# Batch 0's retention in three chains, q scaled on GpSimd and the multiply after the values taken out

## The chip, the cores and the metric

One core of a Trainium2 chip runs the whole kernel in one launch. The metric is the device time of that launch in microseconds; the kernel before takes 803.81 us (median of three runs, 803.64 to 804.98).

## The reference

The program is a retention layer (attention with a decay in place of the softmax) and two feed-forward layers behind it. Shapes: 4 batches, 8 heads, 576 positions, head size 64; then 2304 tokens of width 512.

```
scores = q @ k.T / sqrt(64)
ret    = scores * D            # D[i, j] = gamma_h ** (i - j) for i >= j, else 0
attn   = ret @ v               # heads side by side: x, 2304 x 512
h      = (x @ w1) * (x @ w2) @ w3        # 512 -> 1024 -> 1024
x      = h @ w_out                       # 1024 -> 512
g      = max(x @ w_in, 0) + alpha * min(x @ w_in, 0)   # 512 -> 2048
out    = g @ w_out2                      # 2048 -> 512
```

The feed-forward weights come in float64 and are split on the core into a high and a low float32 part; x is split the same way, and each product is made of three matmuls (high x high, high x low, low x high).

## The kernel before

**Retention.** Heads are treated in pairs, one head on partitions 0 to 63, the other on 64 to 127; a batch has four pairs. Positions go in four chunks of 128 and a tail of 64 (`NCH = 5`). With the decay written as `gamma**i * gamma**-j`, a chunk needs: `scores` (TensorE, L287, L276), a multiply by a mask that holds `gamma**-j` and the causal zeros (VectorE, L291, L279, tiles `rt`, `rte`), `moments` (k times v of the chunk, L302, after the keys were scaled by ScalarE in `prep`, L265), a running state `S` that is aged by `gamma**128` and added to (VectorE, L310, L312; `gc` holds the factors), and `values` (L333: state times q; L342: masked scores times v), both into one PSUM tile `o`. Then `decayed` multiplies `o` by `qs`, which is `gamma**i / 8` for each query position (L349, into the tile `xs`), and `split` makes the high part on ScalarE (L172, `xh`) and the low part on VectorE (L173, `xl`).

The masks, the tail mask and `qs` of all pairs are one tile `per_pair`, 448 columns a pair, loaded pair by pair in `load_pair` for batch 0.

`steps()` returns six steps; step c issues scores of chunk c+1, values of chunk c and moments of chunk c+1. What follows on other engines is put in the list `later` and issued at the next `flush()`.

**Batch 0** runs before anything else, as two chains of two pairs (`r0`, `r1`), interleaved by the list `order` at L448. Sixteen matmuls on zeros come first (L440). Between steps, `ws.tick(n)` advances the weight pieces: each piece has four steps (`_first` on ScalarE L93 and L94, `_second` on VectorE L103 to L108, `_third` on ScalarE L112, `_fourth` on VectorE L116), a tick does at most one step of each kind, and the argument says up to which piece.

**Blocks.** The tokens are then cut into blocks of 512 (`BLOCKS`); `ab_unit(n, c)` multiplies a block's x by column c of w1 and of w2 (two groups of 12 matmuls, L179, tile `ps`; weight pieces 2c and 2c+1). Between the groups a `cycle` function is called: it flushes, advances the retention of the next batch, and then does a weight tick. During the first three columns of block 0 that is batch 1:

```python
r = retention(1)
between = cycle(r, 7 / 6, 1, 6)
for c in range(3):
    ws.until(2 * c + 2)
    ab_unit(0, c, between)
```

`ws.until(n)` ticks until n pieces are finished. The first step of a `retention(b)` is `prep`, so the first call of `between` issues all eight key scalings of batch 1, then a tick; the second issues its first scores and moments, then a tick. Batches 2 and 3 lie in the same way between later columns; there odd pairs are stored with the two heads swapped (`crossed`), and `cross()` rewrites the constants for that.

**Order.** TensorE, ScalarE and SyncE (which issues all DMAs) take their instructions in the order of the program text; VectorE and GpSimd are put in order by the framework's planner. After this part come two larger feed-forward stages (from L557 on), which the change does not touch.

Of the kernel before, what the change touches and what calls it, by code (L numbers as in the profile page):

```python
# [16 lines left out]
P = 128  # L17
# [120 lines left out]
def retention_moe_kernel(ctx: ExitStack, tc, qk, kv, w_out1, w3t, w12, w_in, w_out2, alpha, c_row, c_pair, out):  # L138
# [81 lines left out]
    xsp = pool(pa, "xs", bufs=2, side="left")  # L220
# [31 lines left out]
    class Retention:  # L252
# [14 lines left out]

        def scores(self, c):
# [26 lines left out]
        def moments(self, c):  # L295
# [9 lines left out]
            def state():  # L305
                new = attn.tile([P, NPAIR, D], F32, tag="S", name=f"S{b}_{c}", bufs=3)[:, 0:n]
                if c == 0:
                    nc.vector.tensor_copy(new, st)
                else:
                    nc.vector.tensor_tensor(out=new, in0=self.state[c - 1], in1=gc[:, self.ps].unsqueeze(2)  # L310
                                            .to_broadcast([P, n, D]), op=ALU.mult)
                    nc.vector.tensor_tensor(out=new, in0=new, in1=st, op=ALU.add)  # L312
                self.state = {**(self.state or {}), c: new}
# [3 lines left out]
        def values(self, c):  # L317
# [26 lines left out]
            later.append(lambda: self.decayed(c, o, w))  # L344

        def decayed(self, c, o, w):

            x = xsp.tile([P, NPAIR, CH], F32, tag="x", name=f"xs{self.b}_{c}")[:, 0:self.n, 0:w]
            nc.vector.tensor_tensor(out=x.rearrange("p (i r) w -> p i r w", r=2),  # L349
                                    in0=o[:, :, 0:self.n // 2, 0:w].rearrange("p r i w -> p i r w"),  # L350
                                    in1=qs[:, self.ps, 0:w].rearrange("p (i r) w -> p i r w", r=2), op=ALU.mult)
            t0 = self.b * S + c * CH
            cuts = [0] + [t - t0 for t, _ in BLOCKS if t0 < t < t0 + w] + [w]

            def parts():
                for lo, up in zip(cuts, cuts[1:]):
                    n = (t0 + lo) // 512
                    at = t0 + lo - BLOCKS[n][0]
                    xh, xl = (m[:, self.ps, at:at + up - lo] for m in x_block(n))
                    split(xh, xl, x[:, :, lo:up])  # L360

            later.append(parts)
# [21 lines left out]
    def cross():  # L384

        for p in range(1, NPAIR, 2):
# [3 lines left out]
            in_places(2, p, mtail[:, p], c_pair[:, p, 2 * CH:2 * CH + 64])  # L390

    def load_pair(b, p):
# [10 lines left out]
        if b == 0:  # L403
            nc.sync.dma_start(out=per_pair[:, p], in_=c_pair[:, p])
# [24 lines left out]
    nc.sync.dma_start(out=per_row, in_=c_row)  # L429
    load_pair(0, 0)  # L430
    ws.load_until(1)
    load_pair(0, 1)
    load_pair(0, 2)
# [6 lines left out]
    for _ in range(16):  # L440
        nc.tensor.matmul(warm, idle[:, 0:P], idle[:, :512], start=True, stop=True)
    r0, r1 = Retention(0, [0, 1], psum0), Retention(0, [2, 3], psum0)
    r0.prep([0])
    ws.tick(1)
    r0.prep([1])
    ws.tick(1)
    s0, s1 = r0.steps(), r1.steps()
# [682 lines left out]
```

## Time and profile before

| | |
|---|---|
| median of three runs | 803.81 us |
| profiled execution, span | 801.9 us |
| profiled execution, outside the span | not listed; the median is 1.9 us above the span |
| TensorE busy | 787.0 us, 98% |
| VectorE busy | 498.6 us, 62% |
| ScalarE busy | 348.9 us, 44% |
| GpSimd busy | 0.2 us, four instructions |
| granted clock | 0.8 of full speed in the first 40th of the span, 0.9 or more in all others |
| DMA engines | 0.9 or more busy in the first 40th, 0.8 in the second |

The span runs from the first to the last instruction of one profiled execution. Engine names in rows: PE is TensorE (PEld its weight loads), DVE VectorE, ACT ScalarE, POOL GpSimd, SPq the queue of SyncE. `L291` is line 291 of the kernel before. An arrow in brackets names what ended the idle time before an instruction.

### The profile page before, as it was taken

Reading aid. Unit: us, or ns where it says so; the run is one execution under the profiler, and the core shown is the slowest. Engines: PE = TensorE matmul, PEld = TensorE weight load, DVE = VectorE, ACT = ScalarE, POOL = GpSimd, SP = SyncE. Lnnn points to the kernel's source line nnn. Section 1 sums busy time; section 2 is a strip of 40 time slices with the busy share of each in tenths; the row PEclk is TensorE's granted clock in tenths of the full one; section 3 lists DMA queues with packets and bytes.
Section 4 is the critical chain, followed back from the end, with each engine's and each line's share of the span. In section 5 each row is a group of like instructions: output and inputs, shape, how many; then the busy total and the mean of one; then the engine's idle time right before and its main releaser. Section 6 shows DMA issues by size and latency. Waiting matters only on the chain.

```text
span 801.9 us, 12688 instructions
## 1 busy us (share of the span) xinstructions
PE 787.0 (98%) x4768; PEld 694.4 (87%) x4768; DVE 498.6 (62%) x895; ACT 348.9 (44%) x648; POOL 0.2 (0%) x4
## 2 busy tenths in 40 slices
PE   7899999999999999999999999999999999999998
PEld 4678888888888988999999999999987888888886
DVE  4895785325477799888833677587899923222232
ACT  3453562231255566656514465465666522222121
POOL 0000000000000000000000000000000000000000
PEclk8999999999999999999999999999999999999999
DMA  9843931561366669899916925225557635344341
GB/s 347 343 159 120 345 150 54 166 247 54 116 201 181 201 201 353 285 400 407 381 46 216 358 100 197 109 98 199 184 194 247 209 99 177 106 132 138 99 136 42
DMA packets 81341, 156.24 MB, mean 195 GB/s; under 512 B 9600, under 2 KB 57728, under 8 KB 81280
## 3 DMA queue, kind: packets, MB, share of 16 engines
q1 hardware_dynamic: 81280, 155.43, 55.6%
q8 instruction: 37, 0.61, 0.3%
q14 instruction: 24, 0.20, 0.1%
HBM read 104.02 MB, written 51.38 MB: 194 GB/s over the span
## 4 chain that ended last, share of the span: by engine, by line
PE 90%; DVE 4%; DMA 2%; issue 1%; ACT 1%; SPq 1%; ACTq 0%; DVEq 0%
PE ps L179 25%; PE o L1045 23%; PE h L884 18%; PE y L817 12%; PE pw L631 5%; PE sc L287 2%; PE o L342 2%; PE o L333 1%; PE st L302 1%; DMA kv<-in_kv_dram 1%; DMA xs<-x2d 1%; DMA gr<-gd 0%; DVE gl L173 0%; DVE g L902 0%; DVE g L896 0%
## 5 line engine op out<-in xcount | busy, mean ns | idle before, releaser
L179 PE MATMUL ps<-xh,w 128*128 128x512 f32 (+1 forms) x640 | 186.0, 372 | 0.6 <-DVE w L116 0.3
L1045 PE MATMUL o<-wb,gh 128*128 128x512 f32 x576 | 177.6, 389 | 1.1 <-ACT gh L172 1.1
L179 PEld LDWEIGHTS ps<-xh,w 128*128 128x128 f32 x640 | 116.0, 188 | 22.3 <-DVE w L116 0.7
L1045 PEld LDWEIGHTS o<-wb,gh 128*128 128x128 f32 x576 | 108.1, 188 | 23.8 <-ACT gh L172 1.5
L179 PE MATMUL ps<-xl,w 128*128 128x512 f32 (+1 forms) x320 | 118.0, 369 | 0.0
L1045 PE MATMUL o<-wb,gl 128*128 128x512 f32 x288 | 112.3, 390 | 0.4 <-DVE gl L173 0.4
L173 DVE TENSOR_TENSOR gl<-gr,gh 128x768 fp32r<-128x768 f32 x48 | 45.9, 957 | 100.1 <-ACT gh L172 100.1
L817 PE MATMUL y<-yab,wp 128*128 128x384 f32 x576 | 100.0, 334 | 0.0
L817 PEld LDWEIGHTS y<-yab,wp 128*128 128x128 f32 x576 | 99.9, 188 | 0.1
L172 ACT CAST gh<-gr 128x768 fp32r<-128x768 f32 x48 | 40.2, 838 | 116.5 <-PE o L1045 112.0
L179 PEld LDWEIGHTS ps<-xl,w 128*128 128x128 f32 x320 | 60.4, 189 | 9.8 <-DVE xl L173 0.3
L1045 PEld LDWEIGHTS o<-wb,gl 128*128 128x128 f32 x288 | 54.1, 188 | 12.5 <-DVE gl L173 1.3
L896 DVE SCALAR_TENSOR_TENSOR g<-m,al,g 128x384 f32<-128x384 f32 x48 | 29.7, 618 | 49.3 <-ACT g L895 47.8
L884 PE MATMUL h<-xT,wv 128*128 128x384 f32 x288 | 54.9, 334 | 1.5 <-DVE g L902 1.5
L884 PE MATMUL h<-xT,wu 128*128 128x384 f32 x288 | 55.0, 335 | 0.5 <-ACT h L909 0.3
L884 PEld LDWEIGHTS h<-xT,wv 128*128 128x128 f32 x288 | 50.3, 188 | 1.8 <-DVE g L902 1.8
L108 DVE CUSTOM_DVE_ANT_0 a<-a,b 128x1024 uint16<-128x1024 uint16 x72 | 49.5, 688 | 3.3
L884 PEld LDWEIGHTS h<-xT,wu 128*128 128x128 f32 x288 | 50.2, 188 | 1.1 <-ACT h L909 0.6
L488 ACT CAST ab<-f 128x512 fp32r<-128x512 f32 (+1 forms) x40 | 23.1, 577 | 63.8 <-DVE f L492 59.4
L492 DVE TENSOR_TENSOR f<-f,ps 128x512 f32<-128x512 f32 (+1 forms) x40 | 25.3, 632 | 30.8 <-PE ps L179 30.6
L103 DVE TENSOR_SCALAR a<-a 128x512 f32<-128x512 f32 x72 | 30.4, 422 | 22.3 <-ACT a L93 21.9
L631 PE MATMUL pw<-wo,w 128*128 128x512 f32 x192 | 43.7, 389 | 0.0
(95 smaller groups left out, 1008.8 us busy)
## 6 DMA issues: line engine op xcount, KB each, us to landing
gd<-g SPq DMA_DIRECT2D x96, 192.0 KB, 1.9
gr<-gd SPq DMA_DIRECT2D x96, 192.0 KB, 2.6
abd<-ab SPq DMA_DIRECT2D x32, 512.0 KB, 4.1
raw<-in_w_out_dram SPq DMA_DIRECT2D x24, 512.0 KB, 3.9
yab<-abd SPq DMA_DIRECT2D x24, 384.0 KB, 8.2
raw<-in_w_dram SPq DMA_DIRECT2D x16, 512.0 KB, 6.9
raw<-in_w3t_dram SPq DMA_DIRECT2D x16, 512.0 KB, 4.1
rawi<-in_w_in_dram SPq DMA_DIRECT2D x16, 512.0 KB, 6.1
```

What stands on the lines that cost most here:

```text
L103: nc.vector.tensor_scalar(out=a, in0=a, scalar1=self.LEAST, scalar2=self.MOST, op0=ALU.max, op1=ALU.min)
L108: nc.vector.tensor_tensor(out=a.bitcast(I32), in0=a.bitcast(I32), in1=b, op=ALU.add)
L172: nc.scalar.copy(hi, src)
L173: nc.vector.tensor_tensor(out=lo, in0=src, in1=_f32(hi), op=ALU.subtract)
L179: nc.tensor.matmul(ps, a, bb, start=(n == 0), stop=(n == last))
L488: nc.scalar.copy(t[:, 0], f)
L492: nc.vector.tensor_tensor(out=f, in0=f, in1=pss[1], op=ALU.mult)
L631: nc.tensor.matmul(acc[i], a[:, ic], bb, start=(k == 0 and n == 0), stop=(k == C1 - 1 and n == 2))
L817: nc.tensor.matmul(ys[o], wpc[c][a][:, oc], yab[b, c][:, bb], start=(c == 0 and i == 0), stop=(c == C1 - 1 and i == 2))
L884: nc.tensor.matmul(ps, a[:, x, ks], b[:, y, k], start=(fresh and n == 0), stop=(n == 5), skip_group_check=True)
L896: nc.vector.scalar_tensor_tensor(out=g, in0=r, scalar=neg[:, c:c + 1], in1=g, op0=ALU.mult, op1=ALU.add)
L1045: nc.tensor.matmul(accs[b][i], x[:, m, ic], y, start=(j == 0 and m == 0 and q == 0), stop=(j == C1 - 1 and m == 1 and q == 2))
```

## The change

Batch 0 is run as three chains: pair 0, pair 1, then pairs 2 and 3. The masks are loaded in two transfers of two pairs each, the first ahead of pair 0's data. q is multiplied by `qs` in place on GpSimd before the scores (two instructions a pair), so the PSUM tile `o` already holds the finished x; the multiply L349 and the pool `xs` are gone, and `parts` splits x straight from PSUM. The aging of the state is a GpSimd instruction behind the addition (`aged`), for the chunks that have a successor. For crossed batches `cross()` also rewrites `qs`. Two warm matmuls fewer are issued. In batch 0 weight piece 0 takes its four steps in the first two chains, and weight piece 1 takes all four in the third; before, piece 1 took two there and the other two in `ws.until(2)`. The loads of batch 1's pairs 0 and 1 follow the last step of the second chain.

```diff
@@ -217,7 +217,6 @@
     pa = ExitStack()
     decay = pool(pa, "decay", side="left")
     attn = pool(pa, "attn", side="left")
-    xsp = pool(pa, "xs", bufs=2, side="left")
     early = pool(pa, "early", bufs=2, side="left")
     pb = ExitStack()
     xp = pool(pb, "xp", side="right")
@@ -264,6 +263,14 @@
                 for j in range(2):
                     nc.scalar.activation(k[:, 4 * j:4 * j + 4], k[:, 4 * j:4 * j + 4], AF.Copy,
                                          scale=kd[:, 2 * p + j:2 * p + j + 1])
+
+        def scale(self, pairs=None):
+            for p in pairs or self.pairs:
+                q, by = qt[self.b][p], qs[:, p]
+                full = q[:, 0:512].rearrange("p (c i) -> p c i", i=CH)
+                nc.gpsimd.tensor_tensor(out=full, in0=full, in1=by.unsqueeze(1).to_broadcast([P, 4, CH]),
+                                        op=ALU.mult)
+                nc.gpsimd.tensor_tensor(out=q[:, 512:S], in0=q[:, 512:S], in1=by[:, 0:64], op=ALU.mult)
 
         def scores(self, c):
             b, n = self.b, self.n
@@ -307,10 +314,12 @@
                 if c == 0:
                     nc.vector.tensor_copy(new, st)
                 else:
-                    nc.vector.tensor_tensor(out=new, in0=self.state[c - 1], in1=gc[:, self.ps].unsqueeze(2)
+                    nc.vector.tensor_tensor(out=new, in0=self.aged, in1=st, op=ALU.add)
+                self.state = {**(self.state or {}), c: new}
+                if c < NCH - 2:
+                    self.aged = attn.tile([P, NPAIR, D], F32, tag="aged", name=f"aged{b}_{c}", bufs=2)[:, 0:n]
+                    nc.gpsimd.tensor_tensor(out=self.aged, in0=new, in1=gc[:, self.ps].unsqueeze(2)
                                             .to_broadcast([P, n, D]), op=ALU.mult)
-                    nc.vector.tensor_tensor(out=new, in0=new, in1=st, op=ALU.add)
-                self.state = {**(self.state or {}), c: new}
 
             later.append(state)
 
@@ -341,25 +350,23 @@
                         vj, rj = vt[b][p][rows], rt[rows, m]
                     nc.tensor.matmul(o[pp, p % 2, m // 2, 0:w], vj, rj, start=(c == 0 and m in clears), stop=True,
                                      skip_group_check=True)
-            later.append(lambda: self.decayed(c, o, w))
-
-        def decayed(self, c, o, w):
-
-            x = xsp.tile([P, NPAIR, CH], F32, tag="x", name=f"xs{self.b}_{c}")[:, 0:self.n, 0:w]
-            nc.vector.tensor_tensor(out=x.rearrange("p (i r) w -> p i r w", r=2),
-                                    in0=o[:, :, 0:self.n // 2, 0:w].rearrange("p r i w -> p i r w"),
-                                    in1=qs[:, self.ps, 0:w].rearrange("p (i r) w -> p i r w", r=2), op=ALU.mult)
+            later.append(lambda: self.parts(c, o[:, :, 0:n // 2 or 1, 0:w], w))
+
+        def parts(self, c, o, w):
+
             t0 = self.b * S + c * CH
             cuts = [0] + [t - t0 for t, _ in BLOCKS if t0 < t < t0 + w] + [w]
-
-            def parts():
-                for lo, up in zip(cuts, cuts[1:]):
-                    n = (t0 + lo) // 512
-                    at = t0 + lo - BLOCKS[n][0]
-                    xh, xl = (m[:, self.ps, at:at + up - lo] for m in x_block(n))
-                    split(xh, xl, x[:, :, lo:up])
-
-            later.append(parts)
+            for lo, up in zip(cuts, cuts[1:]):
+                m = (t0 + lo) // 512
+                at = t0 + lo - BLOCKS[m][0]
+                if self.n == 1:
+                    src = o[:, self.pairs[0] % 2, :, lo:up]
+                    xh, xl = (x[:, self.ps, at:at + up - lo] for x in x_block(m))
+                else:
+                    src = o[:, :, :, lo:up].rearrange("p r i w -> p i r w")
+                    xh, xl = (x[:, self.ps, at:at + up - lo].rearrange("p (i r) w -> p i r w", r=2)
+                              for x in x_block(m))
+                split(xh, xl, src)
 
         def steps(self):
             def step(c):
@@ -388,6 +395,7 @@
             for h in range(2):
                 nc.sync.dma_start(out=mask[:, h, p], in_=c_pair[:, p, (1 - h) * CH:(2 - h) * CH])
             in_places(2, p, mtail[:, p], c_pair[:, p, 2 * CH:2 * CH + 64])
+            in_places(2, p, qs[:, p], c_pair[:, p, 2 * CH + 64:])
 
     def load_pair(b, p):
         x = attn.tile([P, 2, S], F32, tag=f"qk{p}", name=f"qk{b}_{p}")
@@ -400,8 +408,6 @@
         else:
             nc.sync.dma_start(out=x, in_=qk[b, p])
             nc.sync.dma_start(out=y, in_=kv[b, p])
-        if b == 0:
-            nc.sync.dma_start(out=per_pair[:, p], in_=c_pair[:, p])
 
     def load_apart(b, p, n):
 
@@ -427,9 +433,11 @@
     first = ExitStack()
     psum0 = attention_psum(first, 2)
     nc.sync.dma_start(out=per_row, in_=c_row)
+    nc.sync.dma_start(out=per_pair[:, 0:2], in_=c_pair[:, 0:2])
     load_pair(0, 0)
     ws.load_until(1)
     load_pair(0, 1)
+    nc.sync.dma_start(out=per_pair[:, 2:4], in_=c_pair[:, 2:4])
     load_pair(0, 2)
     load_pair(0, 3)
     ws.load_until(2)
@@ -437,26 +445,24 @@
     load_apart(1, 2, 10)
     load_apart(1, 3, 13)
     warm = psum0["o"].tile([P, 512], F32, tag="o", name="warm", bufs=2)
-    for _ in range(16):
+    for _ in range(14):
         nc.tensor.matmul(warm, idle[:, 0:P], idle[:, :512], start=True, stop=True)
-    r0, r1 = Retention(0, [0, 1], psum0), Retention(0, [2, 3], psum0)
-    r0.prep([0])
-    ws.tick(1)
-    r0.prep([1])
-    ws.tick(1)
-    s0, s1 = r0.steps(), r1.steps()
-    order = [s0[0], s0[1], s0[2], s0[3], None, s1[0], s0[4], s1[1], s0[5], s1[2], s1[3], s1[4], s1[5]]
-    pieces = {1: 1, 6: 1, 8: 2, 10: 2}
-    for n, step in enumerate(order):
-        if step is None:
-            r1.prep()
-            continue
+    r0, r1, r2 = (Retention(0, pairs, psum0) for pairs in ([0], [1], [2, 3]))
+    s0, s1, s2 = r0.steps(), r1.steps(), r2.steps()
+
+    def ready(r, p):
+        r.scale([p])
+        r.prep([p])
+
+    def loads():
+        load_pair(1, 0)
+        load_pair(1, 1)
+
+    one, two = (lambda: ws.tick(1)), (lambda: ws.tick(2))
+    for step in (lambda: ready(r0, 0), s0[0], one, s0[1], s0[2], one, lambda: ready(r1, 1), s0[3], one, s1[0],
+                 s0[4], one, s1[1], s0[5], s1[2], s1[3], lambda: ready(r2, 2), s1[4], lambda: ready(r2, 3),
+                 s1[5], loads, s2[0], s2[1], two, s2[2], two, s2[3], two, s2[4], two, s2[5]):
         step()
-        if step is s0[-1]:
-            load_pair(1, 0)
-            load_pair(1, 1)
-        if n in pieces:
-            ws.tick(pieces[n])
         flush()
     flush()
     flush()
@@ -517,7 +523,12 @@
 
     def retention(b):
         r = Retention(b, list(range(NPAIR)), psum1)
-        return Steps([r.prep] + r.steps())
+
+        def prep():
+            r.scale()
+            r.prep()
+
+        return Steps([prep] + r.steps())
 
     first_o = ExitStack()
     psum1["o"] = pool(first_o, "ps_o1", space=PSUM, reuse_waits="tile")
```

## Rows read from the trace of the kernel before

**Rows 1.** Stages: time, busy us of engines (count), granted clock, DMA share, GB/s.
```profile
7.40:34.00 26.60, 20.92 (x290) 16.64 (x289) 19.74 (x51) 9.38 (x22) 0.00 (x0) 0.87 1.03 413
...
68.00:110.00 42.00, 41.85 (x194) 34.16 (x190) 28.39 (x53) 24.01 (x47) 0.00 (x0) 1.00 0.78 263
```

**Rows 2.** Waits of 0 to 34 us: total us, times, longest.
```profile
ACT xh L172 <- DVE xs L349: 14.7, 8, 2.7
...
PE sc L287 <- DMA qk<-in_qk_dram: 2.5, 1, 2.5
```

**Rows 3.** VectorE groups of 7.4 to 34 us, shapes apart: busy us, mean ns.
```profile
L291 DVE TENSOR_TENSOR rt<-sc,per_pair 128x512 f32<-128x512 f32 x8 | 5.5, 687 | 0.4 <-DMA per_pair<-const_pair_dram 0.3
L349 DVE TENSOR_TENSOR xs<-o,per_pair 128x256 f32<-128x256 f32 x8 | 3.3, 418 | 1.0 <-PE o L342 0.8
L173 DVE TENSOR_TENSOR xl<-xs,xh 128x256 fp32r<-128x256 f32 x7 | 3.0, 425 | 2.0 <-ACT xh L172 2.0
L310 DVE TENSOR_TENSOR S<-S,per_row 128x128 f32<-128x128 f32 x6 | 1.7, 283 | 0.0
```

**Rows 4.** Timeline of TensorE around batch 1's start, and its first wait.
```profile
10.36 0.80 PE L287 MATMUL sc<-qk 64*128 64x128 f32 x4 [2.46 <-DMA qk<-in_qk_dram]
...
33.90 0.50 PE L179 MATMUL ps<-xh,w 128*128 128x512 f32 x1
...
39.56 0.71 PE L287 MATMUL sc<-qk 64*128 64x128 f32 x8
...
42.24 0.50 PE L179 MATMUL ps<-xh,w 128*128 128x512 f32 x1 [0.18 <-ACT w L112]
...
43.27 0.50 PE L179 MATMUL ps<-xh,w 128*128 128x512 f32 x1 [0.29 <-DVE w L116]
```

**Rows 5.** Timeline of ScalarE, 37.9 to 43.3 us.
```profile
37.91 0.58 ACT L502 COPY f<-ps 128x512 f32<-128x512 f32 x1
38.38 1.71 ACT L265 ACTIVATE kv<-kv,per_row 128x256 f32<-128x256 f32 x4
39.99 1.70 ACT L265 ACTIVATE pair<-pair,per_row 128x256 f32<-128x256 f32 x4
41.59 0.61 ACT L112 CAST w<-a 128x512 fp32r<-128x512 f32 x1
```

**Rows 6.** Timeline of SyncE's DMA issues, batch 1's second pair.
```profile
26.19 0.42 SPq L401 DMA_DIRECT2D qk<-in_qk_dram  x1
26.71 0.37 SPq L402 DMA_DIRECT2D kv<-in_kv_dram  x1
```

**Rows 7.** Those two DMAs: count, KB, us from issue to landing.
```profile
qk<-in_qk_dram SPq DMA_DIRECT2D x1, 576.0 KB, 8.4
kv<-in_kv_dram SPq DMA_DIRECT2D x1, 544.0 KB, 9.2
```

**Rows 8.** Timeline of weight piece 0, first and second step.
```profile
8.98 0.66 ACT L93 ACTIVATE a<-raw 128x512 f32<-128x512 f32 x1 [0.90 <-DMA raw<-in_w_dram]
...
11.43 0.69 DVE L108 CUSTOM_DVE_ANT_0 a<-a,b 128x1024 uint16<-128x1024 uint16 x1
```

**Rows 9.** GpSimd's widest instruction, and VectorE's widest mask multiply.
```profile
0.24 0.10 POOL L1113 MEMSET const-float32-0.0<- 128x1 f32 x1 [0.24 <-issue]
...
41.40 1.22 DVE L291 TENSOR_TENSOR rt<-sc,per_pair 128x1024 f32<-128x1024 f32 x1
```

**Rows 10.** Granted clock from 9 to 17 us, columns as in Rows 1.
```profile
9.00:9.50 0.50, 0.00 (x0) 0.00 (x0) 0.00 (x0) 0.50 (x1) 0.00 (x0) 1.00 0.98 404
9.50:10.00 0.50, 0.00 (x0) 0.00 (x0) 0.33 (x1) 0.50 (x2) 0.00 (x0) 0.77 1.00 411
...
13.00:14.00 1.00, 1.00 (x9) 0.93 (x8) 1.00 (x4) 0.07 (x1) 0.00 (x0) 0.50 1.00 407
...
16.50:17.00 0.50, 0.50 (x8) 0.36 (x8) 0.50 (x3) 0.00 (x0) 0.00 (x0) 0.91 1.00 412
```

**Rows 11.** Key scaling of batches 2 and 3: ns, first and last start.
```profile
L265 ACT ACTIVATE kv<-kv,per_row x16: 497/498/512, 105.0 to 176.7; 128x256 f32<-128x256 f32 x16
```

## The prediction

> **What bounds the kernel now.** I read the table of stages first. From 68 us on TensorE is busy in practically the whole of every stretch (41.85 of 42.0 us in the first one) at the full granted clock [rows 1]; work taken from VectorE or added to GpSimd there is beside it and is worth nothing. The stretch that the change can shorten is 7.4 to 34 us, the retention of batch 0: TensorE 20.92 of 26.6 us, VectorE 19.74, granted clock 0.87 on average, and the DMA engines full (share 1.03, 413 GB/s) [rows 1].
>
> The waits say why it is long. TensorE stands 2.5 us for the second pair's q and k [rows 2, 4]; ScalarE waits 14.7 us in eight places for VectorE's `xs` [rows 2], which is one link of a chain: scores, mask multiply, values, `xs`, `xh`, `xl`, all but three on VectorE. The reader should also see what comes behind: block 0's first matmul is at 33.90, its 24 matmuls end at 39.56 where batch 1's scores begin, and the next weight column starts at 42.24 with its third matmul (the first that needs the low half of the weights) at 43.27 [rows 4]. From there TensorE runs without a wait of note to the end of batch 1. So the change is worth what it does to those two moments, 42.24 and 43.27, and not what it does to 33.90.
>
> **Batch 0 ends earlier.** Removed from VectorE: ten multiplies into `xs` (eight at 0.418, so 3.3 us, and two small ones) and six agings (6 x 0.283 = 1.7) [rows 3]. Added, because pairs 0 and 1 now run alone at half width: eight mask multiplies of 256 columns for four of 512, 8 x 0.42 - 4 x 0.687 = 0.6 (0.42 from the `xs` row, the same shape); eight low halves of 128 columns for four of 256, 8 x 0.283 - 4 x 0.425 = 0.6; up to eight state operations for four, at most 4 x 0.283 = 1.1 [rows 3]. The fourth step of weight piece 1 (0.7, a 512-wide operation as in [rows 3]) moves from behind block 0's start to before it. Net about -2 us of VectorE work, and the chain loses a link per chunk. With nothing else gained the start of block 0 goes from 33.90 to some 31.7; with most of VectorE's idle time in the stretch gone too (26.6 - 19.74 = 6.9 us, of which the first two cannot go), to 27. I take 29.5.
>
> The front of it loses a little, and is hidden. Two masks (448 KB) now stand ahead of pair 0, 224 KB more than before ahead of pair 1: at 413 GB/s [rows 1] 0.55 us for pair 1, so its q and k come at 10.9 for 10.36 [rows 4]. Then GpSimd scales q, 128x512 and 128x64. The trace has no such instruction: GpSimd's four memsets take 0.10 at 128x1, VectorE's multiply 0.69 at 128x512 and 1.22 at double width [rows 3, 9]. Bounds 0.1 and 1.22 a pair for the large part; I take 1.2, the upper one, since the lower is of one column, and 1.5 with the tail. Meanwhile pair 0's four steps fill the time in which TensorE stood 2.46 us. The two warm matmuls fewer cost nothing: TensorE waits for data there.
>
> At this place the rule of the Trainium skill against the change is weighed: GPSIMD Engine Reference, section 4.1 Engine selection, keeps elementwise work with two inputs on VectorE, GpSimd being about twice as slow. By it the estimate is 2 x 0.69 = 1.4 for the large part. No run here shows it yet; the sum would not move by it.
>
> Aging on GpSimd has a whole step of slack: the aged state is wanted when the next chunk's moment is done, one step later, and a step is at least the 0.69 of the mask multiply plus the other VectorE work. Cost nothing, up to 1.22 [rows 9], below a step of two pairs.
>
> **What batch 1 then waits for.** The queue of transfers is full throughout 7.4 to 34 us, and the change leaves its bytes and the order of the later ones as they are. So batch 1's second pair lands when it landed before: q and k at 26.19 + 8.4 = 34.6, keys and values at 26.71 + 9.2 = 35.9 [rows 6, 7]. Before, this was hidden: ScalarE scaled those keys only at 38.38 [rows 5]. Now it is late.
>
> ScalarE runs in the order written. The weight ticks are the second half of it: before, two ticks ran just ahead of block 0 (in `ws.until(2)`), and they did the first step of pieces 2 and 3 and the second step of piece 2. Now the four ticks inside the third chain have finished piece 1, `until(2)` finds nothing to do, and piece 2 begins in the first `between` call, behind the copy L502 and behind the eight key scalings of batch 1. Those are 0.43 each (1.71 for four) [rows 5]. The chain: keys land 35.9; pairs 1, 2 and 3, 6 x 0.43 = 2.58, end at 38.48; first step of piece 2 to the end of its second took 11.43 + 0.69 - 8.98 = 3.14 for piece 0 [rows 8], so 41.62; high half and the matmul 42.24 - 41.59 = 0.65 [rows 4, 5], so 42.27; low half: 0.61 for L112 [rows 5], 0.69 for a 512-wide operation of VectorE [rows 3] and 0.1 for the handovers, third matmul about 43.0. Against 42.24 and 43.27 before: +0.03 and -0.27, so **-0.25**. This holds for any start of block 0 up to 31.7, because L502 waits for half of block 0's 5.66 us (39.56 - 33.90): 31.7 + 2.83 + 0.47 (38.38 - 37.91) + 0.86 is 35.9 [rows 4, 5]. The five microseconds gained before it become a wait. Bounds on the chain: -0.5 if VectorE is free at each step, +1.2 if the planner puts batch 1's mask multiply (1.22 [rows 9]) into it.
>
> GpSimd scales four pairs here. If in order of pairs: from 34.6, three pairs at 1.5 give 39.1 and the last scores at 39.4; 42.27 is not reached before 2.3 us a pair.
>
> **The clock.** From 29.5 + 5.66 = 35.2 to 42.27 TensorE has 7.1 us, and in it only batch 1's first scores and moments, under 2.7 us before, waits included (42.24 - 39.56 [rows 4]). In the trace, TensorE stood still from 7.9 to 10.36, and the granted clock fell inside 9.5 to 10.0 (0.77 there, 0.50 after, so from 2.4 to 1.2 GHz); it was back inside 16.5 to 17.0 (0.91), TensorE having been busy without a gap from 13.0 [rows 4, 10]. By those rows the clock falls again about 40, and comes back after some 3.6 us (16.6 - 13.0) to 6.2 us (16.6 - 10.36) of work at half speed: 1.8 to 3.1 us lost. I take 2.0, near the lower end, since dense matmuls follow here.
>
> **Edits priced at nothing.** Batches 1 to 3 lose `xs` (0.69 each) and agings on VectorE, beside a full TensorE [rows 1]; before batch 2 four more small DMAs pass through SyncE's queue, at the 0.4 of an issue [rows 6] 1.6 us, and batch 2's keys are scaled at 105.0, batch 3's at 176.7 [rows 11], long after their loads; GpSimd's 6 us per batch lies in that slack. PSUM `o` is held for one cast more, with two buffers in batches 0 and 1.
>
> A second rule of the Trainium skill: SBUF — State Buffer, section Who interferes with whom, says that GpSimd and VectorE share a port pair under an exclusive lock. No row shows GpSimd reading. By it VectorE could stand 1.2 us once or twice in batch 0; block 0 would start at 31 for 29.5, still under 31.7, and the sum stays.
>
> **Sum.** Span 801.9 - 0.25 + 2.0 = 803.65; outside the span lie 1.9 us (803.81 - 801.9, the median of the three runs), so 805.6.
>
> **Rivals.**
> 1. *The wait comes, the clock holds.* For it: later in the stretch TensorE waits too and the clock stays. Against: a wait of 2.46 us did bring it down [rows 4, 10], and the one here is longer. 803.81 - 0.25 = 803.6, up to 804.8 with the mask multiply in the chain.
> 2. *Faster: block 0's early start reaches the end.* One mechanism: piece 2 is ready before TensorE wants it, because the keys land earlier or the first step of piece 2 is not behind them. Then the next column follows the last moments: 38.48 + 0.3 = 38.8 for 42.24, -3.4, so 800.4. For it: VectorE and ScalarE have the time. Against: full DMA engines and ScalarE's written order. It decides if piece 2's first step runs before 35.
> 3. *Slower: GpSimd is dear.* Above 2.3 us a pair (three times VectorE's multiply), batch 1's scores set the end: at 3 us a pair 34.6 + 9 + 0.9 = 44.5, +2.2, and the clock falls as well: 808. For it: no row prices GpSimd. Against: VectorE does the same multiply in 0.69 [rows 3], and 2.3 is over three times that.
>
> **How the numbers follow.** Forecast 0.46 (own range 804.8 to 807.2), rival 1 0.25, rival 2 0.17, rival 3 0.12. A measurement can tell about 0.2%, 1.6 us: under 802.2 is faster, over 805.4 slower. Faster: rival 2, 0.17. Slower: 0.36 of the forecast, rival 3, hardly any of rival 1: 0.48. Same: the rest, 0.35. The range 801.0 to 807.6 takes in the forecast, rival 1, the upper half of rival 2 and a third of rival 3.
>
> **What would show it.** In the profile after: block 0's first matmul at 28 to 31.7 (if later than 33, the first step is wrong); ScalarE waiting for batch 1's keys until about 35.9; L93 of piece 2 behind the eight scalings; the next weight column at 42 to 43; the granted clock at 0.5 for some microseconds after it; GpSimd's scaling near 1.2 us. A next column before 40, or a clock of 1.00 throughout 36 to 48 us, makes the prediction wrong.

## The result, and the profile after

The changed kernel takes 815.6 us (median of five runs, 814.28 to 815.71) against 803.81 for the kernel before (five runs, 803.46 to 805.7): ratio 1.0133, 95% interval 1.0115 to 1.015; it is slower by 10.7 us by the ratio, by 11.8 by the medians. The prediction was 805.6. Its sign was right; its size was not, and the time lies outside the predicted range.

Lines have moved: in the kernel after, L264 scales the keys, L271 and L273 scale q, L294 makes scores, L298 is the mask multiply, L309 makes moments, L317 adds to the state, L321 ages it, L342 and L351 make values, L508 copies a group out of PSUM.

The stages first, columns as in [rows 1]. The row 7.4 to 34 answers to the first of [rows 1], 68 to 110 to the second; the rows after them cut the first 58 us finer.

```profile
7.40:34.00 26.60, 24.88 (x239) 18.09 (x240) 17.58 (x44) 9.42 (x25) 13.99 (x22) 0.68 1.02 410
68.00:110.00 42.00, 40.63 (x290) 33.30 (x288) 23.45 (x38) 14.98 (x28) 7.46 (x8) 1.00 0.61 193
...
14.00:16.00 2.00, 2.00 (x22) 1.26 (x20) 1.75 (x3) 0.18 (x1) 1.85 (x3) 0.56 1.03 424
16.00:20.00 4.00, 4.00 (x32) 2.73 (x32) 2.37 (x9) 0.74 (x3) 1.86 (x4) 0.50 1.03 403
28.00:32.00 4.00, 4.00 (x42) 3.37 (x42) 2.93 (x6) 1.50 (x3) 1.36 (x2) 0.59 1.03 425
48.00:50.00 2.00, 0.00 (x0) 0.00 (x0) 2.00 (x4) 0.00 (x0) 0.37 (x1) 0.59 0.00 0
50.00:55.00 5.00, 3.94 (x8) 2.65 (x9) 4.86 (x11) 3.43 (x6) 0.00 (x0) 0.50 0.57 210
```

VectorE is busy 17.58 for 19.74 us in this window, but batch 0 is not over at 34. Up to block 0's first matmul (33.90 before, 37.63 after) it is busy 1.4 us more than before, 21.11 us:

```profile
7.40:37.63 30.23, 27.82 (x289) 20.17 (x289) 21.11 (x52) 10.68 (x28) 16.34 (x25) 0.72 0.99 396
```

The work itself shrank by the 2 us that the prediction took, but wide steps of the weight pieces take twice as long beside GpSimd. VectorE's groups up to block 0, first before, then after:

```profile
L106 DVE SCALAR_TENSOR_TENSOR a<-raw,a 128x512 uint32<-128x512 uint32 x2 | 1.4, 692 | 0.1
```

```profile
L106 DVE SCALAR_TENSOR_TENSOR a<-raw,a 128x512 uint32<-128x512 uint32 x2 | 2.9, 1426 | 0.0
L116 DVE TENSOR_TENSOR w<-a,w 128x512 fp32r<-128x512 f32 x2 | 2.8, 1404 | 0.0
```

L116 takes 0.68 us before. With a small one (L874, 0.85 for 0.18) these give back 3.6 us. TensorE is busier (24.88 for 20.92) and no further: its granted clock is 0.68 of full speed where it was 0.87. It runs at 0.50, that is 1.2 GHz, from about 14.3 to 31 us. Before, the low level lasted from inside 9.5 to 10 to inside 16.5 to 17 [rows 10]. It falls a second time inside 48 to 50 and stays low past 55.

TensorE's timeline, the moments of [rows 4]:

```profile
13.80 0.34 PE L309 MATMUL st<-kv 128*64 128x64 f32 x4 [1.41 <-DVE S L317]
...
37.63 0.50 PE L179 MATMUL ps<-xh,w 128*128 128x512 f32 x1
...
50.90 0.80 PE L179 MATMUL ps<-xh,w 128*128 128x512 f32 x1 [5.82 <-ACT w L112]
...
110.47 0.50 PE L179 MATMUL ps<-xh,w 128*128 128x512 f32 x1 [1.84 <-ACT f L508]
```

Against [rows 4]: block 0 starts at 37.63 for 33.90 (+3.7), the next weight column at 50.90 for 42.24 (+8.7), its second group at 58.71 for 48.34 (+10.4). A stand of 1.84 us at 108 is new. The two, 10.4 + 1.8, make the 12.0 between the spans (813.9 and 801.9) within 0.2: the loss is complete at 111 us, and a stage that starts at 422.2 before starts at 434.2.

At the first stand, at 12.4, TensorE waits for the addition L317, which needs the aged state from GpSimd. GpSimd's timeline:

```profile
10.32 1.52 POOL L271 TENSOR_TENSOR qk<-qk,per_pair 128x512 f32<-128x512 f32 x1 [0.66 <-DMA qk<-in_qk_dram]
11.81 0.76 POOL L273 TENSOR_TENSOR qk<-qk,per_pair 128x64 f32<-128x64 f32 x1
12.54 0.29 POOL L321 TENSOR_TENSOR aged<-S,per_row 128x64 f32<-128x64 f32 x1
```

Pair 0's state is aged behind pair 1's scaling, whose two instructions take 2.28 us, and is ready at 12.83. VectorE, busy without a gap from 9.63 to 13.86, adds it 0.6 us later, behind a step of a weight piece:

```profile
12.85 0.68 DVE L108 CUSTOM_DVE_ANT_0 a<-a,b 128x1024 uint16<-128x1024 uint16 x1
13.45 0.21 DVE L317 TENSOR_TENSOR S<-aged,st 128x64 f32<-128x64 f32 x1
```

So GpSimd's queue and VectorE's order both stand behind it; their shares are not shown. The second stand is read from ScalarE's timeline, whose rows answer to [rows 5]:

```profile
40.69 0.59 ACT L508 COPY f<-ps 128x512 f32<-128x512 f32 x1 [2.68 <-PE ps L179]
41.17 1.71 ACT L264 ACTIVATE kv<-kv,per_row 128x256 f32<-128x256 f32 x4
42.78 1.69 ACT L264 ACTIVATE pair<-pair,per_row 128x256 f32<-128x256 f32 x4
44.38 0.67 ACT L93 ACTIVATE a<-raw 128x512 f32<-128x512 f32 x1
...
50.23 0.62 ACT L112 CAST w<-a 128x512 fp32r<-128x512 f32 x1 [2.99 <-DVE a L108]
```

And from VectorE's, between that L93 and that L112, without a row left out:

```profile
45.08 0.43 DVE L103 TENSOR_SCALAR a<-a 128x512 f32<-128x512 f32 x1 [0.91 <-ACT a L93]
45.42 1.22 DVE L298 TENSOR_TENSOR rt<-sc,per_pair 128x1024 f32<-128x1024 f32 x1
46.55 0.42 DVE L104 TENSOR_SCALAR a<-a 128x512 uint32<-128x512 uint32 x1
46.89 0.42 DVE L315 COPY S<-st 128x256 f32<-128x256 f32 x1
47.22 0.68 DVE L490 TENSOR_TENSOR ab<-f,ab 128x512 fp32r<-128x512 f32 x1
47.82 0.84 DVE L103 TENSOR_SCALAR a<-a 128x512 f32<-128x512 f32 x1
48.58 0.68 DVE L106 SCALAR_TENSOR_TENSOR a<-raw,a 128x512 uint32<-128x512 uint32 x1
49.18 0.41 DVE L104 TENSOR_SCALAR a<-a 128x512 uint32<-128x512 uint32 x1
49.52 0.68 DVE L108 CUSTOM_DVE_ANT_0 a<-a,b 128x1024 uint16<-128x1024 uint16 x1
```

L93 of piece 2 does stand behind the eight key scalings, as predicted, but these start when the copy L508 lets them (41.17), not when their transfer lands. And the chain from L93 to the end of L108 takes 5.82 us for the 3.14 of piece 0 [rows 8]: between its four VectorE steps lie the mask multiply, a state copy, the product's split L490 and two steps of piece 3 (from start to start 1.13, 0.33, 0.60, 0.76 and 0.34: 3.16 us).

### The profile page after: what moved, and what is told of

It reads as the page before. It is cut to its first block, busy times and chain, and to the rows that moved or that the text cites. A ratio compares the mean times of both kernels' runs of the same rounds, so it can differ in the third digit from the quotient of the medians.

```text
span 813.9 us, 12770 instructions
## 1 busy us (share of the span) xinstructions
PE 795.0 (98%) x4766; PEld 698.6 (86%) x4766; DVE 490.1 (60%) x869; ACT 349.2 (43%) x653; POOL 37.6 (5%) x54
## 4 chain that ended last, share of the span: by engine, by line
PE 88%; DMA 4%; DVE 3%; SPq 2%; ACT 2%; issue 1%; ACTq 0%; DVEq 0%
PE o L1056 23%; PE h L895 21%; PE ps L179 21%; PE y L828 12%; PE pw L642 5%; PE sc L294 2%; PE o L351 2%; DMA raw<-in_w_dram 2%; SPq L389 1%; PE o L342 1%; DMA kv<-in_kv_dram 1%; DMA gr<-gd 1%; PE st L309 1%; DVE a L106 0%; DVE a L108 0%
## 5 line engine op out<-in xcount | busy, mean ns | idle before, releaser
L172 ACT CAST gh<-gr 128x768 fp32r<-128x768 f32 x48 | 40.1, 836 | 117.0 <-PE o L1056 113.9
L108 DVE CUSTOM_DVE_ANT_0 a<-a,b 128x1024 uint16<-128x1024 uint16 x72 | 50.7, 705 | 3.4
L498 DVE TENSOR_TENSOR f<-f,ps 128x512 f32<-128x512 f32 (+1 forms) x40 | 25.3, 632 | 44.9 <-PE ps L179 44.6
L93 ACT ACTIVATE a<-raw 128x512 f32<-128x512 f32 x56 | 37.8, 674 | 14.4 <-DMA raw<-in_w_dram 8.0
```

The costliest lines, as they stand in the source:

```text
L93: nc.scalar.activation(a, raw.bitcast(F32).rearrange("p (n w) -> p n w", w=2)[:, :, 1], AF.Abs)
L108: nc.vector.tensor_tensor(out=a.bitcast(I32), in0=a.bitcast(I32), in1=b, op=ALU.add)
L172: nc.scalar.copy(hi, src)
L498: nc.vector.tensor_tensor(out=f, in0=f, in1=pss[1], op=ALU.mult)
```

## Experiments

Every ratio is to the kernel before on the same chip, with a 95% interval. "Column" is the first matmul of the next weight column (42.24 before, 50.90 after), "second group" that of its second half (48.34 and 58.71). Runs of several versions spread over 4 us or more, so where a single profile and a median differ, the median is taken. The diffs are cut to the lines that tell the edit; dots mark what is left out.

**1. The last two ticks of the third chain taken out.**

```diff
-  ... s2[2], two, s2[3], two, s2[4], two, s2[5]):
+  ... s2[2], two, s2[3], s2[4], s2[5]):
```

> Only the weight ticks are put back: two of the four ticks of the third chain go, so that the steps of pieces 2 and 3 that ran ahead of block 0 before run there again. Theory A (the late first step of piece 2 is the largest loss): block 0 still starts near 37.6, but the next weight column comes 8.3 us behind it as before (42.24 - 33.90) and not 13.3 (50.90 - 37.63), so no 5.8 us stand, no clock fall at 48, some 2 us more: about 815.6 - 7 = 808.5. Rival B (the column is late because VectorE's chain is stretched by other work or by GpSimd, wherever it begins): still 11 us or more behind block 0, 814 to 816.

Measured 806.74, ratio 1.0024 (1.0006 to 1.0041). Block 0 starts as late as in the kernel after (37.76), yet nothing stands for piece 2. TensorE's timeline at the column, with no wait in brackets:

```profile
45.17 0.50 PE L179 MATMUL ps<-xh,w 128*128 128x512 f32 x1
```

`until(2)` now does the first steps of pieces 2 and 3 ahead of the copy (L93 at 38.56 and 39.71, L264 at 41.30). So 8.8 us (ratios) or 8.9 (medians) go with two ticks. The clock of batch 0 did not move with them, in the table of stages:

```profile
16.00:30.00 14.00, 14.00 (x122) 10.19 (x122) 7.15 (x22) 3.29 (x12) 6.45 (x11) 0.50 1.03 412
```

**2. The aging back on VectorE**, the rest as after.

```diff
-  nc.gpsimd.tensor_tensor(out=self.aged, in0=new, ...
+  nc.vector.tensor_tensor(out=self.aged, in0=new, ...
```

> Only the aging of the state goes back to VectorE. Theory C (in batch 0 the aged state stood behind the q scaling in GpSimd's queue, TensorE stood 1.4 us for it at 12.4 to 13.8, the clock fell there and stayed at 0.5 to 31): no such wait, clock up through batch 0, block 0 starts at 30 to 33 for 37.6, and the total is 810 to 812, since the late weight column stays. Rival D (chains of one pair are too thin for the clock whatever the aging does): the clock falls all the same, block 0 at 36 to 38, 814 to 816.

Measured 817.88, ratio 1.0161 (1.0123 to 1.02): no gain, and the idea that the aging's place holds the clock down fell. Block 0 starts at 40.23, later than either theory put it. TensorE still stands 0.97 and 1.13 us (at 11.81 and 14.43) for VectorE's `S`, and the clock is 0.50 from 16 to 28. The stands now come from VectorE, whose L104 (0.42 elsewhere) takes 1.45 beside GpSimd's scaling. VectorE's timeline:

```profile
10.17 1.45 DVE L104 TENSOR_SCALAR a<-a 128x512 uint32<-128x512 uint32 x1
```

GpSimd's of the same moment:

```profile
10.08 1.26 POOL L271 TENSOR_TENSOR qk<-qk,per_pair 128x512 f32<-128x512 f32 x1 [2.52 <-DMA qk<-in_qk_dram]
```

L104 ends at 11.62, 0.28 after GpSimd's instruction, as if it did its work only when the other was done.

**3. Two chains with the order and the ticks of before**, the rest as after. The loop over `order` in the diff of the change is restored, with `scale` beside each `prep`:

```diff
-  r0, r1, r2 = (Retention(0, pairs, psum0) for pairs in ([0], [1], [2, 3]))
+  r0, r1 = Retention(0, [0, 1], psum0), Retention(0, [2, 3], psum0)
...
+  pieces = {1: 1, 6: 1, 8: 2, 10: 2}
```

> Batch 0 again in two chains of two pairs with the ticks and the order of before; q scaled and state aged on GpSimd, x from PSUM, masks first as in the change. Rival D: the clock is back by 17 as before, block 0 at 33 to 35, 803 to 806. Theory C: the aged state still stands behind the scalings, the clock stays low past 20, block 0 at 35 to 37, 806 to 809.

Measured 812.47, ratio 1.0084 (1.0057 to 1.011; the profiled run is the fastest, 808.55), far above the forecast of the theory, though the clock is back inside 16 to 18 (0.79), as before. A new stand takes its place, and the clock falls again behind it (0.66 in 38 to 42). TensorE's timeline:

```profile
36.68 0.45 PE L342 MATMUL o<-qk,S 64*64 64x64 f32 x8 [4.48 <-DVE S L317]
```

And GpSimd's:

```profile
34.41 1.26 POOL L271 TENSOR_TENSOR qk<-qk,per_pair 128x512 f32<-128x512 f32 x1 [1.22 <-DMA qk<-in_qk_dram]
35.63 0.32 POOL L273 TENSOR_TENSOR qk<-qk,per_pair 128x64 f32<-128x64 f32 x1
35.91 0.40 POOL L321 TENSOR_TENSOR aged<-S,per_row 128x128 f32<-128x128 f32 x1
```

Batch 0's last aging stands in GpSimd's queue behind two scalings of batch 1, which wait for their transfers. GpSimd takes its instructions in the order that the planner wrote. In the kernel after the same queue has a part in the 1.41 us at 12.4.

**4. The crossed `qs` loaded early**, into a tile of their own (`qx`, from which the crossed pairs are then scaled), with batch 1's loads.

```diff
-  in_places(2, p, qs[:, p], c_pair[:, p, 2 * CH + 64:])   # in cross()
+  for p in (1, 3):                                         # with the first loads
+      in_places(2, p, qx[:, p // 2], c_pair[:, p, 2 * CH + 64:])
```

> The crossed copies of qs for batches 2 and 3 get a tile of their own, loaded with the first loads; the four small DMAs ahead of batch 2's loads go. Theory E (these four delay the loads of the next weights by 2 us, and TensorE's 1.84 us stand at 108 comes from that): the stand goes, 813 to 814. Rival: the stand at 108 comes from the late column in batch 1 alone and stays, 815 to 816.

Measured 814.56, ratio 1.01 (1.0074 to 1.0126). The stand at 108 is gone (TensorE 40.00 of 40 us in 70 to 110, for 38.63). The medians give 1.0 us; the intervals overlap, so no gain in time is shown.

**5. Experiments 2 and 3 together**: two chains, the aging on VectorE; both diffs as above.

> Batch 0 in two chains with the ticks of before, and the aging on VectorE; q still scaled on GpSimd, x from PSUM, masks first. Theory F (in the two-chain run TensorE stood 4.48 us at 32 because the aged state of batch 0 stood in GpSimd's queue behind the scaling of batch 1's q, which waits for its DMA): the stand goes, block 0 starts at 31 to 33, total 800 to 804. Rival (the stand comes from the moments or from VectorE): it stays, 808 to 813.

Measured 806.82, ratio 1.0036 (1.0018 to 1.0054). The stand of 4.48 is gone, block 0 starts at 32.93 and the column at 40.34, so GpSimd's queue was the cause there. But 800 to 804 was not reached. The early column waits at its third matmul, in TensorE's timeline:

```profile
42.15 0.73 PE L179 MATMUL ps<-xh,w 128*128 128x512 f32 x2 [1.08 <-DVE w L116]
```

Of the 1.9 us at the column 1.1 are left at that matmul (43.27 before), and a stand of 2.0 us for the copy of `f` (L511 there) comes at 97, where the kernel after has its own at 108. With the multiply off VectorE (the aging is back there) block 0 starts 1 us earlier in the chains of before; the waits of TensorE name the reason, 3.8 us for GpSimd's scaled q, where before it stood 2.5 for the transfer [rows 2].

**6. Matmuls on zeros against the clock**: experiment 1 with two 128x512 matmuls into a free PSUM bank in each step of the one-pair chains.

```diff
   self.scores(c + 1)
+  if self.b == 0 and self.n == 1 and c >= 0:
+      for _ in range(2):
+          nc.tensor.matmul(fill, idle[:, 0:P], idle[:, :512], start=True, stop=True)
```

> The ticks put back as in a1_ticks, and two 128x512 matmuls on zeros into an unused PSUM bank in every step of the two one-pair chains, between the scores and the values. Theory D (one pair does not cover the latency of its own mask multiply, so TensorE is not busy enough for its clock): granted clock 1.0 before 22 us, block 0 starts at 32 to 35 for some 36 to 37, 803 to 805. Rival (the clock is held down by something else): 0.5 to 30 as before, and the added work costs 9 x 2 x 0.43 = 7.7 us there, 811 or more.

Measured 804.76, ratio 1.001 (0.9996 to 1.0023); TensorE's work was raised and block 0 starts 3.7 us earlier (34.10 for 37.76). The row of the stages to set beside that of experiment 1:

```profile
16.00:28.00 12.00, 12.00 (x135) 6.94 (x134) 6.03 (x20) 3.37 (x12) 5.46 (x11) 1.00 1.04 412
```

Both show TensorE busy in the whole stretch, at 0.50 there and 1.00 here. The stand at 13 (1.41 us in 1) is gone too, so the matmuls fill a gap as well as the steps.

**7. Experiment 5 with the early `qs` of 4**; its diff is that of 4.

> b1_two_age with the crossed copies of qs loaded early in a tile of their own. Theory E (four small DMAs ahead of batch 2's loads delay the weights behind them): 1 to 2 us under b1_two_age. Rival (there is slack for them): the same as b1_two_age within 0.5.

Measured 805.22, ratio 1.0018 (1.0003 to 1.0032); no stand in 70 to 110 (40.00 of 40). By the medians of 4 and this one the four DMAs that the prediction priced at nothing cost 1.0 and 1.6 us, in overlapping intervals both times. In this profile the clock falls in two-pair chains too: behind stands of 0.99 and 1.40 us it is at 0.50 from 22 to 28 and back at 29, and block 0 starts at 35.32.

**8. Experiment 5 with the masks loaded per pair** and 16 warm matmuls, as before.

```diff
-  nc.sync.dma_start(out=per_pair[:, 0:2], in_=c_pair[:, 0:2])
...
+  if b == 0:                      # in load_pair, behind the pair's keys and values
+      nc.sync.dma_start(out=per_pair[:, p], in_=c_pair[:, p])
...
-  for _ in range(14):
+  for _ in range(16):
```

> b1_two_age with the masks loaded pair by pair as before and 16 warm matmuls. If the order of the masks matters: q of pair 0 lands 1.1 us earlier, but its scaling waits for the mask behind it, so the start is later by 0.3 to 1 and the total with it. If it does not (the second pair's q is what TensorE waits for): within 0.5 of b1_two_age.

Measured 805.82, ratio 1.0027 (1.0016 to 1.0039), not told apart from 5: the masks' place and the two warm matmuls show no loss in the time. The masks' place does move batch 0: the second pair's scores start at 13.61 for 11.55 in 5, and block 0 at 35.26 for 32.93.

**9. Nothing on GpSimd in batch 0**: experiment 1 with batch 0's scaling and aging on VectorE.

```diff
-  nc.gpsimd.tensor_tensor(out=full, ...
+  eng = nc.gpsimd if self.b else nc.vector
+  eng.tensor_tensor(out=full, ...
```

> The three chains with the ticks put back, and no GpSimd work in batch 0: its q scaling and its aging run on VectorE, the other batches as changed. Theory D (chains of one pair are too thin, whoever does the scaling): the granted clock still lies at 0.5 for ten microseconds or more between 10 and 30, 805 to 809. Rival G (GpSimd's queue and its collisions with VectorE at 10 to 14 us brought the clock down, and without them it holds): 1.0 from 18 at the latest, block 0 before 34, 802 to 804.

Measured 808.38, ratio 1.0067 (1.0043 to 1.009). The clock falls all the same, in the stages:

```profile
16.00:28.00 12.00, 11.56 (x100) 8.42 (x96) 6.98 (x28) 3.24 (x11) 3.10 (x4) 0.53 1.03 407
```

So GpSimd is not needed for the fall; with two-pair chains (3, 5) the clock was back by 18 us, with one-pair chains it is not, and the two-pair chain that follows brings it back only at about 30. VectorE's group that took 1.43 us beside GpSimd is back at 0.69, so it was GpSimd that stretched it:

```profile
L106 DVE SCALAR_TENSOR_TENSOR a<-raw,a 128x512 uint32<-128x512 uint32 x2 | 1.4, 686 | 0.0
```

**10. One matmul on zeros a step** for the two of experiment 6.

```diff
-      for _ in range(2):
+      for _ in range(1):
```

> As b2_fill with one matmul on zeros a step for two. If one is enough to hold the clock: block 0 some 2 us earlier than with two (9 x 0.21), at 32, total 803 to 804.5. If not: 0.5 for ten microseconds again, 805.5 to 807.5.

Measured 804.5, ratio 1.0002 (0.9986 to 1.0017): one is enough (1.00 from 14 to 32), block 0 starts at 32.73, and of the stand at 13 0.87 us are left.

**11. Experiments 10 and 4 together, with `ws.tick(6)`** ahead of the first column, to begin piece 2 sooner.

```diff
   ws.until(2 * c + 2)
+  if c == 0:
+      ws.tick(6)
```

> A version meant to beat both: c4_fill1, the crossed copies of qs loaded early, and one more weight tick ahead of block 0, so that piece 2's third step stands ahead of batch 1's key scaling. My theory of the second stretch says that the gain before block 0 is kept only if the next column's weights are ready before that scaling: column 1 of block 0 then starts right behind batch 1's first moments, 39 to 41 for 42.24, total 800 to 803. Rival (batch 1's start is bound by its loads and scaling, and the tick only moves the wait): 803 to 805.

Measured 816.98, ratio 1.017 (1.0145 to 1.0196): missed by far. The next one separates the tick.

**12. That tick alone in the kernel before.**

> The kernel before with nothing but that one more weight tick ahead of block 0. It separates the tick from the rest of c1_best. By the trace of before TensorE stands 0.2 and 0.3 us for piece 2 at 42.24 and 43.27, behind waits for the keys; so a gain of 0.3 to 0.8 at most, 803.0 to 803.8; or a loss of up to 1 if ScalarE's added step delays block 0's own pieces.

Measured 814.17, ratio 1.0135 (1.0113 to 1.0156). The tick brings piece 2's third step, L112, ahead of the copy and the key scalings in ScalarE's written order, and L112 waits for VectorE. ScalarE's timeline:

```profile
39.21 0.62 ACT L112 CAST w<-a 128x512 fp32r<-128x512 f32 x1 [1.47 <-DVE a L108]
...
40.87 0.56 ACT L502 COPY f<-ps 128x512 f32<-128x512 f32 x1
41.33 1.70 ACT L265 ACTIVATE kv<-kv,per_row 128x256 f32<-128x256 f32 x4
```

The copy comes 3 us later than in [rows 5], and the second group 3.5 us later (51.86 for 48.34). A second stand comes at 97, in TensorE's timeline:

```profile
99.61 0.80 PE L179 MATMUL ps<-xh,w 128*128 128x512 f32 x1 [2.82 <-ACT f L502]
```

That copy stands in ScalarE's order behind an L93 that waits for its transfer until 97.36. The clock falls at both places, in the stages:

```profile
42.00:46.00 4.00, 3.58 (x18) 2.38 (x19) 3.83 (x7) 4.00 (x10) 0.00 (x0) 0.80 0.44 173
...
70.00:110.00 40.00, 37.03 (x185) 29.86 (x180) 25.36 (x48) 18.66 (x35) 0.00 (x0) 0.91 0.74 247
```

The second fall lasts from 99 to about 105.6 us (0.50). One tick more costs the kernel before 10.9 us, about as much as two ticks spent in batch 0 cost the kernel after; how the tick leads to the stand at 97 no run tests.

**13. The changed kernel, ticks and all, with the one matmul on zeros of 10.** It asks whether the two large losses are one.

> The changed kernel with one 128x512 matmul on zeros per step of the one-pair chains, which held the granted clock at 1.00 in batch 0 when the ticks were those that cost nothing; here the ticks stay as the change has them. It asks whether the two losses add or whether the clock's is the root of the other. Theory H (the root): with block 0 at about 32 the copy and the key scalings of batch 1 are no longer late, the scalings end with their transfer near 38.5, L93 of piece 2 stands there (44.38 in the changed kernel), and with the stretched chain of 5.85 us the next column is at 44.5 to 45; as predicted, the clock then falls there. 50.9 - 44.7 is 6 us back: 807 to 810, between the prediction and the result. If the chain is the predicted 3.14 us, the column is at 42.3 and the time 804.5 to 806.5. Theory A alone (the ticks cost 9 us whatever the clock): 812 to 814.

Measured 810.22, ratio 1.0079 (1.0057 to 1.0102): 4.3 us back by the ratios, 5.4 by the medians, 0.2 above the range of theory H, with the column where it put it. TensorE's timeline:

```profile
32.60 0.50 PE L179 MATMUL ps<-xh,w 128*128 128x512 f32 x1
...
44.95 0.79 PE L179 MATMUL ps<-xh,w 128*128 128x512 f32 x1 [4.92 <-ACT w L112]
```

ScalarE's:

```profile
35.65 0.59 ACT L512 COPY f<-ps 128x512 f32<-128x512 f32 x1 [2.68 <-PE ps L179]
...
39.34 0.66 ACT L93 ACTIVATE a<-raw 128x512 f32<-128x512 f32 x1
...
44.28 0.62 ACT L112 CAST w<-a 128x512 fp32r<-128x512 f32 x1 [2.09 <-DVE a L108]
```

Two of its stages:

```profile
16.00:24.00 8.00, 8.00 (x91) 4.96 (x90) 3.97 (x18) 3.10 (x11) 4.16 (x8) 1.00 1.04 409
...
44.00:46.00 2.00, 1.04 (x3) 0.54 (x3) 1.97 (x5) 1.72 (x3) 0.00 (x0) 0.54 0.00 0
```

With the clock of batch 0 held, everything up to the column moves 5 to 6 us forward; the stand for L112 stays (4.92 us), and so does the second fall of the clock.

**14. Experiments 10 and 4 without the extra tick**; the diffs of 1, 4 and 10.

> The change without its last two ticks of the third chain, with one matmul on zeros per step of the one-pair chains, and the crossed qs loaded early into a tile of their own. Each part removed a loss alone: 9 us, 2 us, 1 to 2 us. If they add up: 801.5 to 803.5, the first version ahead of the kernel before, by 0.1 to 0.3%. Rival: the next column's third matmul waits for the same thing as in the kernel before (43.27 there), batch 1's transfers and ScalarE's order set it, and the time is that of the kernel before, 803.5 to 805.

Measured 804.93, ratio 1.0012 (1.0 to 1.0024). The parts do not add up to a gain: the third matmul of the column, at 43.06 (43.27 before), waits 2.00 us for `DVE w L116`, with the column at 40.32. Loading `qs` early brings no gain over 10 here. No version run here beats the kernel before; 6 and 10 are not told apart from it.

## Why the prediction was wrong

**Batch 0 ends earlier: the step that failed.** It put block 0 at 29.5; it started at 37.63. Two errors, in opposite views:
- *The clock was taken as before.* The prediction let pair 0's steps fill the stand of 2.46 us [rows 4] and asked for the clock only behind block 0. The one-pair chains keep TensorE busy by the page and yet leave it at 1.2 GHz: 10.69 of 10.69 us busy at 0.50 from 14.5 to 25.19, where the chain of two pairs begins. Behind some 6 us of that the clock is back at 31, 17 us after it fell (18.00 of 18 us busy in 14 to 32 us, at 0.53 on average). Experiments 6, 10 and 13 hold the clock with added matmuls alone and move block 0 by 3.7 to 5.0 us; 9 shows that GpSimd is not needed for the fall. So in these runs the one-pair chains alone do not bring the clock back, and one matmul more a step keeps it. Whether it would have fallen without the stand at 13 is not shown: the added matmuls shorten that stand too (1.41 us to 0.85 in 13, 0.87 in 10, none in 6).
- *VectorE's idle time was taken for the room.* With the clock held, block 0 starts at 32.60 to 32.73, and with the old chains at 32.93: 1 to 1.3 us gained for the 4.4 predicted. In experiment 13 TensorE is then itself busy, 17.62 of 18 us in 14 to 32 us, the zeros' matmuls included; in 5 it waits 3.8 us for GpSimd's scaled q. Neither was in the prediction's sum for block 0. VectorE's 2 us less were right as work, but GpSimd stretched other steps by 3.6 us, so VectorE's time up to block 0 grew by 1.4.

**What batch 1 then waits for: right in kind, mis-sized twice.** Piece 2 begins behind the eight scalings; experiment 1 removes just that and gets 8.9 us. But the prediction let the scalings end with their transfer, at 38.48, for any block 0 up to 31.7. Block 0 was later, and its copy set them: they ended at 44.38 after, and at 39.34 in experiment 13. With 37.63 for block 0 the prediction's own sum has them end at 44.37. And the chain was priced from a piece alone on VectorE: 3.14 us, +1.2 at most for the mask multiply. It took 5.82, and 4.91 in experiment 13 (39.34 to the end of L108 at 44.25). With 39.34 and 4.91 in the prediction's sum the column comes at 44.9 (measured there: 44.95) for the 42.27 forecast. Of the 8.6 us by which the kernel after misses that 42.27, the late scalings are 5.9 (44.38 for 38.48) and the chain 2.7.

**The clock behind block 0: right, but later.** It fell inside 48 to 50, for about 40, in the stand for the column, and, by the rows of after (0.59 in 48 to 50, 0.50 from 50 to 55), the 3.94 us that TensorE worked in that stretch at half speed lost some 2 us; 2.0 was forecast.

**GpSimd's price: right; its queue and its neighbour: wrong.** The large part takes 1.26 to 1.52 us (1.2 taken). By the Trainium skill, GPSIMD Engine Reference, section 4.1 Engine selection, two-input work is about twice as slow there; 1.26 to VectorE's 0.687 [rows 3] is 1.8, so the trace agrees. Aging was given a whole step of slack, but nothing was asked of the instructions ahead of it in GpSimd's own queue: 4.48 us of stand in experiment 3, a part of the 1.41 after. The prediction had named an exclusive lock, taken 1.2 us once or twice for it and let it move block 0 alone. The 1.45 us of L104 in experiment 2 is what SBUF — State Buffer, section Who interferes with whom, of the Trainium skill tells: the one that comes second waits for the whole instruction of the first. It reaches back too: GpSimd's tail L273 took 0.76 for 0.32 at 11.81. Up to block 0 VectorE's steps were stretched by the 3.6 us above; what that costs the whole kernel no run measures alone.

**Edits priced at nothing.** The masks' order and the warm matmuls: right in the time, by experiment 8, though the order moves batch 0 by 2 us. The later batches' GpSimd work: no stand names it. cross()'s DMAs: not nothing in the profile, open in the time. In the queue of SyncE they push the loads behind them (batch 2's first is issued 8.4 us behind the first of cross(), 5.9 before); ScalarE waits 7.75 us for piece `raw` at 108.02, and TensorE 1.84 for the copy behind that. Without them that stand is gone (4, 7); but 3, 6, 10 and 13 keep them and stand 0.34 us at most there, so what they cost depends on what else is late, and the 1.0 and 1.6 us of the medians are not clear of the noise.

**The account.** The large losses are not independent. By the ratios, taking the ticks out gives 8.8 us, holding the clock 4.3, both together (experiment 10) 10.5, and not 13.1. The late start of block 0 and the late piece lie on one chain, and part of the first is given back when the second goes. What stays open: how much of the 8.8 is the stand and how much the second fall of the clock. Open too is a fall of the clock at 600 to 640 us in the profiled runs of 1, 4, 6, 10, 11 and 13 and in no other (0.91 over 20 us in 10 and 13, so 1.8 us, 20 x 0.09). Each time it begins within some 2 us behind a stand of TensorE for `gh` (L172), 1.26 us in 10 and 2.62 in 13; but the same stand is 1.12 us before and 2.24 in 5 without a fall, and no experiment touched it.

**Rivals.** Rival 3, 808 by a dear GpSimd, did not occur: batch 1's pairs took 1.26 + 0.32 (experiment 3), the dearest in batch 0 2.28 (after), and the clock and the ticks made the loss. Rival 1 fell with the clock's second fall. That block 0's early start reaches the end (rival 2) failed even where it was brought about: with the column 2 us early (experiments 5, 10, 14) the low half of the weights, L116, was the next thing late.

## What to carry to other kernels

Before a chain is split into thinner ones, ask what TensorE does in it per microsecond: a busy share of 100% that stays at a granted clock of 0.5, here for 11 us, hints at work too thin, and a cheap matmul on zeros in each step tests within one run what the clock costs (it fills short waits as well). Where an engine takes its instructions in a written order, a step moved by one place, early or late, is priced by what then stands behind it, and a chain by what shares its engine at that moment. Work moved to a queue that also holds instructions waiting for transfers inherits their waits, and work moved from VectorE to GpSimd can come back as longer VectorE instructions: compare VectorE's time up to the same event, not in the same window.

## What the hardware showed that was not expected

- Chains of one pair, matmuls of at most 128 columns, filled TensorE to 10.69 of 10.69 us (after, 14.5 to 25.19) and did not bring the clock back from 1.2 GHz; one 128x512 matmul on zeros a step kept it at 2.4 GHz (experiment 10).
- A VectorE instruction of 0.42 us beside a GpSimd one of 1.26 took 1.45, and GpSimd's own 128x64 multiply 0.76 for 0.32. Two 128x512 steps of a weight piece took 1.43 and 1.40 us on average for 0.69 and 0.68; with nothing on GpSimd both were back (experiment 9).
- In the kernel before with one weight tick more, TensorE stood 2.82 us at 97 and was at 0.50 from 99 to 105 us, some 60 us behind the place where the tick was put (experiment 12).
